# A planner's priorities replaced by searched offsets per kind of operation, in a kernel whose five engines follow one written-out plan

## The chip, the cores and the metric

One core of one Trainium2 chip. The metric is device time in microseconds (us) of one execution; the kernel before took 943.68 us as the median of three runs (940.2, 943.68, 949.0). Its profiled execution, from which all rows below come, is another one: 950.11 us, with a span of 948.3 us from the first to the last instruction.

## The reference

Two branches read the same 2048 tokens of 448 channels, float32, and are summed with the input:

```python
x = A_q
xn = _layernorm(x, axis=-1)
return x + _A_ref(xn, A_k, A_v, A_shift_k, A_ssm_k, A_ssm_D) + _B_ref(xn, B_w_q, B_k1, B_k2, B_u, B_v)
```

Branch A is `xn * y`, where `y` is a causal convolution over all 2048 steps, channel by channel (computed with Fourier transforms of length 4096), of the product of a 4-tap convolution of `k` and `v`. Branch B is a lookup among 4096 experts by 16 heads:

```python
s1 = einsum("nhd,ed->nhe", q1, k1); s2 = einsum("nhd,ed->nhe", q2, k2)   # 64 + 64 scores per head
# the best 2 + 2, then the best 2 of the 4 sums -> 2 experts per head, softmax g
act = _gelu(einsum("nd,nhkd->nhk", xf, u[top_e]))
out = einsum("nhk,nhk,nhkd->nd", g, act, v[top_e])
```

So each token reads 32 rows of `u` and 32 of `v`, 65,536 rows of 3,584 bytes in all when both are kept side by side.

## The kernel before

**Tiles and batches.** The tokens are 16 tiles of 128. Of each tile the 32 experts of a token are taken in 8 *batches*, 128 batches in all. A batch is four gathers (line 536, on GpSimd), each of 128 rows of 3,584 bytes, into one of 5 places of `ring`. Then VectorE multiplies the four with the normalized tokens, which TensorE has spread into `xs` (`prod`, line 569); ScalarE sums each of the four products over the channels (`sum`, four times line 575) and applies gelu (line 577); GpSimd makes the coefficients (`co` line 583, `coef` line 582; from batch 104 on VectorE does so, `LATE`); and TensorE adds the weighted rows to `pv` (`val`, line 588). A place of the ring is free for the gathers of batch b when `val` of batch b-5 has read it. After 8 batches `pv` and the tile's input, loaded into `fo`, are added (`res` line 605 and `fold`) and stored.

**Experts' choice.** At the start the query weights are folded with the keys, head by head (`weights`: load `wq`, `pw` line 365, `ws`, `pt`, `whi`, `wlo`). For each tile `turn` transposes the tokens, `score` makes the scores, 4 times 11 matmuls (lines 427 to 431), VectorE finds maxima and their places (`mx`, `mi`, lines 436 and 443) and `pick` makes the indices (`idx`) and gates (`gat`, both line 512) that the gathers need.

**Convolution.** Its 112 groups of 4 channels go in two parts, 28 groups (while the scores run) and 84 groups (after them). Each part has three stages: `in0` and `in1` (`conv_in`: load 4 groups, line 305; the taps, lines 638 to 644; transforms `ps1`, line 655), `sp0` and `sp1` (`spectrum`: `psf` line 699 or 703, `hh`, products `pr` line 720 and `y` lines 727 and 728; `inverse`: `psu` lines 746 to 749, `tw` lines 767 and 771) and `out0` and `out1` (`conv_out`: `psz` line 789, `zt`, `fin` line 796, `gate` and `gateG` lines 807 and 812). The gated result of tiles 0 to 13 is added to the stored rows by 14 accumulating transfers from GpSimd (`accum`, line 944); tiles 14 and 15 add it in `fo` (`add`, line 951).

**What sets the order.** Every step is recorded by `op(engine, duration, function, reads, writes, key)`. `Plan.solve` then lets time run with those durations: whenever an engine is free it takes, of the operations whose inputs are ready, the one with the smallest `key`. The start times that come out give one order for the whole program, and each engine executes its own part of it strictly in that order, waiting at an instruction until its inputs are there. The keys are due times: `tb(b)` for batch b, `due(T)` for the scores of tile T, `span(name, f)` for the fraction f of a stage of the convolution, each with a small constant. GpSimd's gathers and other operations alternate where both are ready. Three banks of PSUM are handed out in the planned order. A gather also waits for the matmul that the plan has ended by 0.5 us before it (`o.pace`).

The functions that the change touches:

Of the kernel before, what the change touches and what calls it, by code (L numbers as in the profile page):

```python
# [18 lines left out]
S, D, H, E = 2048, 448, 16, 64  # L19
# [62 lines left out]


class Op:
    __slots__ = ("eng", "dur", "fn", "deps", "users", "key", "acq", "rel", "nb", "start", "end", "name", "left", "avail", "pace", "last")


class Slot:
# [3 lines left out]
class Plan:  # L92
# [4 lines left out]

    def __init__(self):
        self.ops, self.writer, self.readers = [], {}, {}
        self.free = {}  # L100

    def pool(self, name, n):
# [2 lines left out]
    def op(self, eng, dur, fn, r=(), w=(), key=0.0, acq=None, rel=None, nb=0.0, name="", after=()):  # L105
        o = Op()
        o.eng, o.dur, o.fn, o.key, o.acq, o.rel, o.nb, o.name = eng, dur, fn, key, acq, rel, nb, name
        o.deps, o.users, o.start, o.pace, o.last = set(after), [], None, None, None
        for k in r:
            if k in self.writer:  # L110
                o.deps.add(self.writer[k])
            self.readers.setdefault(k, []).append(o)
        for k in w:
            if k in self.writer:
                o.deps.add(self.writer[k])
            o.deps.update(self.readers.get(k, ()))
# [117 lines left out]
def one_pass(ctx, tc, x, wq, kk, uv, kvh, cst1, cst2, fq, out, flag):  # L234
# [214 lines left out]
    def pick(T, b0, b1, key, two=1):  # L449
# [59 lines left out]
        def put(dst, k):  # L509
            o = bank[s.i][:, :8 * nj].rearrange("p (r k u j) -> p k u r j", r=4, k=2, u=two)[:, k]  # L510
            J = slice(0, NB) if two > 1 else slice(2 * b0, 2 * b1)
            nc.scalar.activation(dst[:, T % 8:T % 8 + two, :, J], o, AF.Copy)
        tiles = [(T + u) % 8 for u in range(two)]
        half = range(4) if two > 1 else range(b0, b1)
        op("ACT", 0.2 + 0.008 * n, lambda: put(idx, 0), r=["pl"], w=[("idx", t, i) for t in tiles for i in half], key=key, name="idx")
        op("ACT", 0.2 + 0.008 * n, lambda: put(gat, 1), r=["pl"], w=[("gat", t, i) for t in tiles for i in half], key=key, rel=("bank", s), name="gat")


    landed = []
# [40 lines left out]
    def batch(T, j):  # L560
        b = NB * T + j
        k = tb(b)
        U = ring[:, b % RING, :, :D]
        aw = sm[:, 4 * (b % 4):4 * (b % 4) + 4]
        ge = sm[:, 16 + 4 * (b % 4):20 + 4 * (b % 4)]
        co = sm[:, 32 + 4 * (b % 4):36 + 4 * (b % 4)]
        u = [("U", b % RING, r) for r in range(4)]
        m = 4
        op("DVE", dve(m * D), lambda: nc.vector.tensor_mul(U[:, :m, :], U[:, :m, :], xs[:, :m, :D]), r=["xs"], w=u[:m], key=k, name="prod")  # L569
        for r in range(m, 4):  # L570
            op("DVE", 0.78, lambda r=r: nc.vector.scalar_tensor_tensor(U[:, r, :], xs[:, r, :D], 1.0, U[:, r, :], op0=ALU.mult, op1=ALU.mult,
                                                                      accum_out=aw[:, r:r + 1]),
               r=["xs"], w=[u[r], ("aw", b % 4, r)], key=k, name="dot")
        for r in range(m):
            op("ACT", 0.575, lambda r=r: nc.scalar.activation(U[:, r, :], U[:, r, :], AF.Copy, accum_out=aw[:, r:r + 1]),  # L575
               w=[u[r], ("aw", b % 4, r)], key=k, name="sum")
        op("ACT", 0.2, lambda: nc.scalar.activation(ge, aw, AF.Gelu_apprx_tanh), r=[("aw", b % 4, r) for r in range(4)], w=[("ge", b % 4)], key=k, name="gelu")

        ve, en, d0, d1 = (nc.vector, "DVE", 0.17, 0.3) if b >= LATE else (nc.gpsimd, "POOL", 0.22, 0.41)

        def coef():
            last_val(ve.tensor_mul(cc[b % 3], co[:, :, None].broadcast_to([P, 4, 32]), rep[:, None, :].broadcast_to([P, 4, 32])).ins, b - 3)  # L582
        op(en, d0, lambda: ve.tensor_mul(co, ge, gat[:, T % 8, :, j]), r=[("ge", b % 4), ("gat", T % 8, j // 2)], w=[("co", b % 4)], key=k - 40.0, name="co")
        op(en, d1, coef, r=[("co", b % 4), "c1"], w=[("cc", b % 3)], key=k - 40.0, name="coef")

        def val():
            for r in range(4):
                v = nc.tensor.matmul(pv[32 * r:32 * r + 32, :D], cc[b % 3][:, r, :], ring[:, b % RING, r, D:],  # L588
                                     start=(j == 0), stop=(j == NB - 1), tile_position=(0, 32 * r)).ins
                tc.declare_no_dep(v, group=GROUP + "s", reason="the coefficients come from all four gathered slots")  # L590
                if r < 3:
                    tc.add_to_no_dep_group(GROUP, v)
            vins[b] = v.name
        op("PE", 1.0, val, r=[("cc", b % 3)] + ([("pv", j - 1)] if j else []), w=[("V", b % RING, r) for r in range(4)] + [("pv", j)] + (["pv"] if j == 0 else []), key=k, name="val")


    ob = [S1[:, 0:D], S1[:, D:2 * D]]

    def fold(T):
        k = tb(NB * T + NB) + 1.0  # L600
        o = fo[:, :]
        last = NB * T + NB - 1
        load(o, x[T], MB * D, ["fo"], k - 12.0, nb=k - 16.0, name="xr")
        if T < T_OUT0:
            op("PE", 0.85, lambda: nc.tensor.matmul(pv[:, :D], ident, o, start=False, stop=False), r=["fo", "c1", ("pv", 0)], w=[("pv", NB)], key=k - 2.0, name="res")
            op("ACT", act(D), lambda: last_val(nc.scalar.activation(o, pv[:, :D], AF.Copy).ins, last), r=[("pv", j) for j in range(NB + 1)], w=["fo", "pv"], key=k, name="fold")
        else:
            op("DVE", dve(D), lambda: last_val(nc.vector.tensor_add(o, o, pv[:, :D]).ins, last), r=[("pv", j) for j in range(NB)], w=["fo", "pv"], key=k, name="fold")
        return o, k
# [167 lines left out]
    def conv_out(p, c, n, tc0, gv, k):  # L777
# [24 lines left out]
        def fv():  # L802
# [1 line left out]
        xv = XA[:, :, ch].rearrange("p t (c k) -> p t c k", k=CH)  # L804
        reads = [("fin", hf) for hf in range(len(halves))]
        wk = [("x", t) for t in range(tc0)]
        op("DVE", dve(CH * n * tc0), lambda: nc.vector.tensor_mul(xv[:, :tc0], fv()[:, :tc0], xv[:, :tc0]), r=reads, w=wk, key=k,
           rel=None if tc0 < NT else ("bank", s), name="gate")
        if tc0 < NT:
            def gg():  # L810
                return gv[0]()[:, :, gv[1] + CH * c:gv[1] + CH * (c + n)].rearrange("p t (c k) -> p t c k", k=CH)
            op("DVE", dve(CH * n * (NT - tc0)), lambda: nc.vector.tensor_mul(gg(), fv()[:, tc0:], xv[:, tc0:]), r=reads + [("x", t) for t in range(tc0, NT)],
               w=[("G", p)], key=k, rel=("bank", s), name="gateG")


    norm(0, 1, 1.0)
# [26 lines left out]
            pick(T - 1, 0, 4, k + 8.0, 2)  # L843

    def conv_first(name, parts):
        tot, done = sum(PARTS[p][1] for p in parts), 0
        for p in parts:
            for c in range(0, PARTS[p][1], BC):
                conv_in(p, c, span(name, done / tot))
                done += BC  # L850

    def conv_mid(name, parts):
        for ka in range(17):
            qs = [ka, 32 - ka] if ka < 16 else [16]
# [168 lines left out]
```

## Time and profile before

| | us |
|---|---|
| median of three runs | 943.68 |
| profiled execution | 950.11 |
| its span | 948.3 |
| GpSimd busy | 606.9 |
| TensorE busy (matmuls) | 707.8 |
| VectorE busy | 679.5 |
| ScalarE busy | 542.9 |
| idle time of GpSimd ahead of gathers | 300.2 |

The page of the profile gives busy time for each engine (PE is TensorE, PEld its weight loads, DVE VectorE, ACT ScalarE, POOL GpSimd, SP the engine that issues the plain loads and stores). A table by windows gives the same for stretches of the span, with the granted share of TensorE's clock and the share of time in which the 16 DMA engines carried packets. The view of waits sums the idle time ahead of a group of instructions by what ended it. The timeline lists instructions with start and duration. "Line" is always a line of the kernel before; the change moves line 305 to 339, 536 to 570, 569 to 603, 588 to 622 and so on.

### The profile page before, as it was taken

The page shows a single profiled execution, that of the slowest core. Times are in us where ns is not written, and L with a number is a line of the kernel's source. Part 1 is how long each engine was busy: PE and PEld are TensorE (multiplying, and loading weights), DVE is VectorE, ACT ScalarE, POOL GpSimd, SP SyncE. Part 2 cuts the span into 40 slices and gives each one's busy share as a digit, 9 for nine tenths or more (in the row PEclk, how much of TensorE's full clock was granted, in tenths as well). Part 3 has the DMA queues.
Part 4 walks back from the last instruction along what each step waited for, and adds up shares of the span by engine and source line. Part 5 has one row for each costly group of instructions (what it writes and reads, how often), then busy time and mean ns, then how long its engine had stood idle before and what let it go on. Part 6 is the DMA issues. An engine that isn't in the chain of part 4 may idle for free.

```text
span 948.3 us, 13985 instructions
## 1 busy us (share of the span) xinstructions
PE 707.8 (75%) x4070; PEld 412.8 (44%) x4070; DVE 679.5 (72%) x1592; ACT 542.9 (57%) x1800; POOL 606.9 (64%) x754
## 2 busy tenths in 40 slices
PE   4777688677868898879888685666677988877671
PEld 2343455444535565546465453443333433344440
DVE  3479786788757887778777856777778999944451
ACT  2346275545554556656473475556577887855551
POOL 0036567688756765665657577787876776665564
PEclk9887779799878998889979778778789999987855
DMA  9998668788978887897779879999999899988898
GB/s 327 327 345 321 189 216 293 250 306 290 320 255 304 301 273 265 289 325 245 246 272 334 291 261 338 365 341 369 345 324 312 295 322 330 325 294 301 290 284 189
DMA packets 72214, 281.46 MB, mean 297 GB/s; under 512 B 10816, under 2 KB 35648, under 8 KB 72128
## 3 DMA queue, kind: packets, MB, share of 16 engines
q0 software_dynamic: 42976, 238.13, 73.5%
q1 hardware_dynamic: 29152, 42.35, 13.2%
q8 instruction: 34, 0.56, 0.2%
q14 instruction: 52, 0.43, 0.1%
HBM read 273.55 MB, written 6.88 MB: 296 GB/s over the span
## 4 chain that ended last, share of the span: by engine, by line
PE 29%; DVE 19%; issue 18%; POOL 12%; DMA 10%; ACT 7%; another core or an unknown queue 3%; SPq 0%; DVEq 0%; POOLq 0%; ACTq 0%
POOL ring L536 9%; DMA ring<-in_uv_dram,idx 8%; PE pv L588 5%; DVE SC L436 5%; DVE ring L569 5%; PE bank L655 4%; ACT ring L575 3%; PE bank L427 2%; PE bank L796 2%; DMA R<-in_wq_dram 2%; PE bank L428 2%; PE bank L429 2%; POOL cc L582 2%; DVE SC L443 2%
## 5 line engine op out<-in xcount | busy, mean ns | idle before, releaser
L536 POOL DMA_INDIRECT ring<-in_uv_dram,idx x512 | 506.9, 990 | 300.2 <-issue 95.4
L575 ACT ACTIVATE ring<-ring 128x448 f32<-128x448 f32 x512 | 288.5, 567 | 85.6 <-DVE ring L569 70.2
L569 DVE TENSOR_TENSOR ring<-ring,xs 128x1792 f32<-128x1792 f32 x128 | 257.4, 2016 | 95.6 <-DMA ring<-in_uv_dram,idx 81.5
L588 PE MATMUL pv<-ring,cc 128*32 128x448 f32 x1024 | 145.4, 650 | 69.8 <-POOL cc L582 34.4
L436 DVE MAX8 SC<-bank 128x8 f32<-128x64 f32 x512 | 118.5, 231 | 47.9 <-PE bank L431 21.7
L655 PE MATMUL bank<-c,S 128*64 128x132 f32 x896 | 77.5, 329 | 30.8 <-ACT ring L575 8.8
L427 PE MATMUL bank<-WR,xh 128*128 128x512 f32 x192 | 89.4, 466 | 10.9 <-DVE xl L416 4.9
L575 ACT ACTIVATION_READ_ACCUMULATOR ring<-ring 128x1 f32 x512 | 97.1, 190 | 0.0
L655 PEld LDWEIGHTS bank<-c,S 128*64 128x64 f32 x896 | 63.7, 165 | 65.3 <-ACT ring L575 24.4
L429 PE MATMUL bank<-WR,xl 128*128 128x512 f32 x192 | 82.7, 431 | 3.1 <-issue 2.5
L428 PE MATMUL bank<-WR,xh 128*128 128x512 f32 x192 | 82.8, 431 | 0.8 <-DVE WR L386 0.8
L588 PEld LDWEIGHTS pv<-ring,cc 128*32 128x32 f32 x1024 | 22.3, 116 | 122.6 <-POOL cc L582 46.0
L703 PE MATMUL bank<-x1b,S 128*128 128x336 f32 x132 | 51.6, 496 | 12.6 <-ACT x1b L767 5.0
L427 PEld LDWEIGHTS bank<-WR,xh 128*128 128x128 f32 x192 | 40.5, 211 | 42.0 <-issue 17.5
L659 ACT ACTIVATE x1b<-bank 128x264 f32<-128x264 f32 x84 | 30.8, 388 | 44.0 <-PE bank L655 32.5
L714 ACT ACTIVATE S<-bank 64x112 f32<-64x112 f32 x132 | 34.0, 257 | 37.1 <-PE bank L699 16.3
L443 DVE FIND_INDEX8 SC<-SC,bank 128x8 uint32<-128x256 f32 x128 | 52.7, 424 | 0.0
L720 DVE TENSOR_TENSOR S<-bank,S 128x224 f32<-128x224 f32 (+1 forms) x66 | 40.5, 618 | 13.8 <-issue 4.0
L582 POOL TENSOR_TENSOR cc<-sm,c 128x128 f32<-128x128 f32 x104 | 48.2, 463 | 3.3
L746 PE MATMUL bank<-S,c 128*128 128x112 f32 x264 | 42.0, 322 | 6.7 <-issue 2.7
L429 PEld LDWEIGHTS bank<-WR,xl 128*128 128x128 f32 x192 | 40.6, 211 | 14.3 <-issue 2.9
L365 PE MATMUL bank<-R 128*64 128x448 f32 x128 | 31.8, 631 | 19.7 <-DMA R<-in_wq_dram 15.6
(130 smaller groups left out, 1020.1 us busy)
## 6 DMA issues: line engine op xcount, KB each, us to landing
R<-in_wq_dram SPq DMA_DIRECT2D x16, 896.0 KB
S<-in_kvh_dram SPq DMA_DIRECT2D x28, 400.0 KB
ring<-in_uv_dram,idx POOLq DMA_INDIRECT x512
S<-in_fq_dram SPq DMA_DIRECT2D x66, 64.0 KB
fo<-in_x_dram SPq DMA_DIRECT2D x16, 224.0 KB
out_dram<-fo SPq DMA_DIRECT2D x16, 224.0 KB
out_dram<-XA POOLq DMA_DIRECT2D x14, 224.0 KB
XA<-in_x_dram SPq DMA_DIRECT2D x2, 1344.0 KB
```

The source lines that it names most:

```text
L427: nc.tensor.matmul(o, xh[:, c, :], wh[:, c, ns], start=(c == 0), stop=False)
L428: nc.tensor.matmul(o, xh[:, c, :], wl[:, c, ns], start=False, stop=False)
L429: nc.tensor.matmul(o, xl[:, c, :], wh[:, c, ns], start=False, stop=False)
L436: nc.vector.max(mx[:, 8 * n + j, :] if safe else m2[:, m, 2 * j:2 * j + 8], bank[s.i][:, 64 * j:64 * j + 64])
L443: nc.vector.max_index(m4i[:, 2 * m + g, :], m2[:, m, 8 * g:8 * g + 8], bank[s.i][:, 256 * g:256 * g + 256])
L536: g = nc.gpsimd.indirect_dma_start(dst, None, uv, bass.IndirectOffsetOnAxis(ap=idx[:, T % 8, r, j:j + 1], axis=0)).ins
L569: op("DVE", dve(m * D), lambda: nc.vector.tensor_mul(U[:, :m, :], U[:, :m, :], xs[:, :m, :D]), r=["xs"], w=u[:m], key=k, name="prod")
L575: op("ACT", 0.575, lambda r=r: nc.scalar.activation(U[:, r, :], U[:, r, :], AF.Copy, accum_out=aw[:, r:r + 1]), w=[u[r], ("aw", b % 4, r)] ...
L582: last_val(ve.tensor_mul(cc[b % 3], co[:, :, None].broadcast_to([P, 4, 32]), rep[:, None, :].broadcast_to([P, 4, 32])).ins, b - 3)
L588: v = nc.tensor.matmul(pv[32 * r:32 * r + 32, :D], cc[b % 3][:, r, :], ring[:, b % RING, r, D:], start=(j == 0), stop=(j == NB - 1), tile_ ...
L655: nc.tensor.matmul(o[64 * i:64 * i + 64, w * j:w * j + w], src, f1[:, i, :], start=True, stop=True, tile_position=(0, 64 * i))
L703: op("PE", 0.95 * n / 448 + 0.05, lambda t=t, sl=sl: nc.tensor.matmul(bank[sl.i][:, :n], fmb[u], x1[p][:, :, q, t, :], start=True, stop=True),
```

## The change: four offsets for each kind of operation

Each operation gets a group, its name and, in the convolution, its stage (`psf@sp1`). For 94 groups a table `RANK` holds four numbers. Over the keys that the group has in the kernel, from its smallest to its largest, the four numbers are interpolated linearly and added to the key. Durations, `solve`, tiling, buffers and every instruction stay. Three dependencies are added that follow the written order wherever keys could now turn it round: `gat` after `idx`, `gateG` after `gate`, and the last `val` of a tile after `res`. Loading `fo` and `res` move out of `fold` into `residual`, which is recorded after the tile's first batch.

```diff
+RANK = {
+    "DMAc1": (-94.0, -79.0, 73.0, 37.0), "DMAc2": (-7.0, 6.5, 6.5, 7.5), ...
+    "DMAkk": (-103.0, -41.0, -70.5, -15.5), "DMAkvh@in0": (-81.5, -81.5, -84.5, -13.0), ...
+    "gather": (1331.0, 1476.0, 2096.5, 2406.5), "gelu": (-52.5, -91.0, -73.5, -120.5), ...
...
+}
@@ pick
-        op("ACT", 0.2 + 0.008 * n, lambda: put(idx, 0), ...)
-        op("ACT", 0.2 + 0.008 * n, lambda: put(gat, 1), ...)
+        ahead = op("ACT", 0.2 + 0.008 * n, lambda: put(idx, 0), ...)
+        op("ACT", 0.2 + 0.008 * n, lambda: put(gat, 1), ..., after=(ahead,), name="gat")
@@ batch
-        op("PE", 1.0, val, r=[("cc", b % 3)] + ([("pv", j - 1)] if j else []), ...)
+        op("PE", 1.0, val, r=[("cc", b % 3)] + ([("pv", j - 1)] if j else []) + ([("pv", NB)] if j == NB - 1 and T < T_OUT0 else []), ...)
@@ experts
             batch(T, j)
+            if j == 0:
+                residual(T)
@@ one_pass, before the plan is solved
+    for o in pl.ops:
+        if o.group in RANK:
+            (a, b), v = ends[o.group], RANK[o.group]
+            w = (o.key - a) / (b - a) * (len(v) - 1) if b > a else 0.0
+            i = min(len(v) - 2, int(w))
+            o.key = o.key + (v[i] * (1 - (w - i)) + v[i + 1] * (w - i))
```

Every engine's order changes, mostly over short distances. Three places follow at which the prediction looks.

The first is the start of SP's queue, which issues the loads: `c` are constants, `XA` tokens (128x448 is one tile), `kk` the keys, `wq` the query weights of a head. Before:

```order
L305 DMA c_67<-in_cst_dram 128x269
L305 DMA XA<-in_x_dram 128x448
L305 DMA R_92<-in_kk_dram 128x256
L305 DMA R_92<-in_wq_dram 128x4x448 x4
L305 DMA XA<-in_x_dram 128x448
L305 DMA XA<-in_x_dram 128x2x448
L305 DMA XA<-in_x_dram 128x6x448 x2
L305 DMA R_92<-in_wq_dram 128x4x448 x8
```

and with the change:

```order
L339 DMA XA<-in_x_dram 128x448 x2
L339 DMA c_67<-in_cst_dram 128x269
L339 DMA XA<-in_x_dram 128x2x448
L339 DMA R_92<-in_wq_dram 128x4x448 x4
L339 DMA R_92<-in_kk_dram 128x256
L339 DMA XA<-in_x_dram 128x6x448 x2
L339 DMA R_92<-in_wq_dram 128x4x448 x6
```

Three tiles of tokens moved ahead of the weights, and the keys behind the first four heads.

The second is VectorE where the second part of the convolution goes from `in1` to `sp1`. Before, from the product of batch 88 (`ring<-ring,xs`) on; 128x1024 to 128x4x64 are the taps of four groups, 128x448 is the `fold` of a tile, and 128x672 with two of 64x336 the products of a spectrum:

```order
L569 TENSOR_TENSOR ring<-ring,xs 128x4x448
L638 TENSOR_TENSOR S_72<-S_72 128x1024
L639 TENSOR_TENSOR S_72<-S_72 128x4
L642 TENSOR_TENSOR S_72<-S_72 128x4x128
L643 TENSOR_TENSOR S_72<-S_72 128x4x64
L644 TENSOR_TENSOR S_72<-S_72 128x4x64
L608 TENSOR_TENSOR fo<-fo,pv 128x448
L569 TENSOR_TENSOR ring<-ring,xs 128x4x448 x2
L720 TENSOR_TENSOR S_72<-bank_84,S_72 128x672
L727 TENSOR_TENSOR Y<-S_72 64x336
L728 TENSOR_TENSOR Y<-S_72 64x336
```

With the change, from the product of batch 86 on:

```order
L603 TENSOR_TENSOR ring<-ring,xs 128x4x448
L677 TENSOR_TENSOR S_72<-S_72 128x1024
L678 TENSOR_TENSOR S_72<-S_72 128x4
L681 TENSOR_TENSOR S_72<-S_72 128x4x128
L682 TENSOR_TENSOR S_72<-S_72 128x4x64
L683 TENSOR_TENSOR S_72<-S_72 128x4x64
L603 TENSOR_TENSOR ring<-ring,xs 128x4x448 x2
L759 TENSOR_TENSOR S_72<-bank_84,S_72 128x672
L766 TENSOR_TENSOR Y<-S_72 64x336
L767 TENSOR_TENSOR Y<-S_72 64x336
L647 TENSOR_TENSOR fo<-fo,pv 128x448
```

The last taps moved from batch 88 to batch 86, and the first spectrum from behind batch 90 to behind batch 88.

The third is the end of GpSimd's queue, gathers and accumulating transfers (`out_dram<-XA`). Before:

```order
L582 TENSOR_TENSOR cc_75<-sm,c_67 128x128
L536 DMA ring<-in_uv_dram,idx 128x896 x83
L944 DMA out_dram<-XA 128x448
L536 DMA ring<-in_uv_dram,idx 128x896
L944 DMA out_dram<-XA 128x448
L536 DMA ring<-in_uv_dram,idx 128x896
L944 DMA out_dram<-XA 128x448
L536 DMA ring<-in_uv_dram,idx 128x896
L944 DMA out_dram<-XA 128x448 x11
```

and with the change:

```order
L570 DMA ring<-in_uv_dram,idx 128x896
L616 TENSOR_TENSOR cc_75<-sm,c_67 128x128
L570 DMA ring<-in_uv_dram,idx 128x896 x87
L991 DMA out_dram<-XA 128x448 x14
```

The last three gathers moved ahead of the first accumulating transfer.

More of the change, by code (lines that the diff above doesn't have):

```diff
@@ L84 @@
 class Op:
-    __slots__ = ("eng", "dur", "fn", "deps", "users", "key", "acq", "rel", "nb", "start", "end", "name", "left", "avail", "pace", "last")
+    __slots__ = ("eng", "dur", "fn", "deps", "users", "key", "acq", "rel", "nb", "start", "end", "name", "left", "avail", "pace", "last", "group")
 class Slot:
@@ L99, in __init__ @@
         self.ops, self.writer, self.readers = [], {}, {}
+        self.stage = ""
         self.free = {}
@@ L108, in op @@
         o.deps, o.users, o.start, o.pace, o.last = set(after), [], None, None, None
+        o.group = name + self.stage
         for k in r:
@@ L216 @@
 LEAD = 0.5
+RANK = {
+    "DMAc1": (-94.0, -79.0, 73.0, 37.0), "DMAc2": (-7.0, 6.5, 6.5, 7.5), "DMAfm@sp0": (30.0, 7.0, -47.0, -79.5), "DMAfm@sp1": (73.5, 60.5, 36.0, 65.5),
+    "DMAkk": (-103.0, -41.0, -70.5, -15.5), "DMAkvh@in0": (-81.5, -81.5, -84.5, -13.0), "DMAkvh@in1": (-191.5, -155.5, -149.0, -60.0),
+    "DMAwq": (-349.0, -13.0, -74.5, -56.0), "DMAx": (-60.0, -81.0, -76.5, -62.0), "DMAxr": (-53.0, -70.5, -83.0, -83.0),
+    "E": (42.0, -43.5, -42.5, -60.0), "SPc1": (-21.5, -0.5, -69.5, 79.5), "SPc2": (11.0, -5.0, 25.0, -46.0), "SPfm@sp0": (-65.0, -64.0, 57.0, -59.5),
+    "SPfm@sp1": (10.0, 10.0, 10.0, 10.0), "SPkk": (34.0, -18.5, -60.0, -42.5), "SPkvh@in0": (-3.5, -22.5, 12.5, 12.5),
+    "SPkvh@in1": (-2.5, 13.0, 28.0, 46.5), "SPwq": (12.0, -0.5, 0.0, 5.5), "SPx": (-101.0, -66.0, -1.0, 130.5),
+    "SPxr": (-145.5, -112.0, -137.0, -134.0), "accum": (-82.0, -105.5, -82.0, -92.0), "accumD": (23.5, 8.0, -32.0, 8.0),
+    "add": (-135.0, -70.5, -116.0, -106.0), "bad": (-32.5, -27.0, -36.0, 6.5), "co": (-0.5, -164.5, -973.5, -827.5),
+    "coef": (60.5, 162.5, -318.0, -288.5), "es": (37.0, 13.0, 31.0, 21.0), "fin@out0": (-10.5, -10.5, -10.5, -10.5),
+    "fin@out1": (-20.5, 44.0, 31.0, -1.5), "flag": (-91.5, -120.0, -136.5, -221.0), "fold": (59.0, 10.0, 142.5, 122.5),
+    "gat": (-8.0, -41.5, -41.5, 1.0), "gate@out0": (-55.5, -102.5, -55.5, 26.0), "gate@out1": (-37.5, -27.0, -27.5, 11.0),
+    "gateG@out0": (-148.0, -206.0, -16.0, -29.5), "gateG@out1": (29.0, 93.5, 26.0, 63.5), "gated": (-57.5, -43.0, -164.5, -244.0),
+    "gather": (1331.0, 1476.0, 2096.5, 2406.5), "gelu": (-52.5, -91.0, -73.5, -120.5), "hh@sp0": (-133.5, -173.5, -144.5, -233.5),
+    "hh@sp1": (-72.0, -91.5, -56.0, -48.0), "idx": (-183.0, -101.0, -44.5, -92.5), "join": (-131.5, -45.0, -25.5, -24.5),
[7 rows of a table added]
+    "sc": (1.0, 1.0, -0.0, 6.5), "spread": (-3.0, -43.5, -104.5, 12.0), "stats": (138.0, 123.5, 136.5, 91.0), "store": (117.5, 205.5, 234.5, 276.0),
+    "storeD": (35.5, 39.0, -18.0, -91.5), "sum": (-13.5, -3.5, -14.0, -3.5), "tap1@in0": (7.0, -69.0, -47.0, -47.0),
+    "tap1@in1": (0.0, -11.0, 0.0, 0.0), "tap2@in0": (-99.5, -114.5, -86.0, -78.5), "tap2@in1": (-99.0, -62.5, -76.5, -36.5),
+    "taps@in0": (-16.0, -3.0, 22.0, -1.5), "taps@in1": (163.0, 251.0, 69.0, 52.5), "th": (1.0, -3.0, -40.5, -40.5), "tw@sp0": (26.0, 11.0, 43.0, 3.0),
+    "tw@sp1": (-17.0, 56.5, 50.5, -145.5), "val": (30.0, 0.5, 3.5, 48.5), "whi": (-362.0, -283.5, -250.0, -143.0),
[4 rows of a table added]
+}
@@ L514, in pick @@
         half = range(4) if two > 1 else range(b0, b1)
-        op("ACT", 0.2 + 0.008 * n, lambda: put(idx, 0), r=["pl"], w=[("idx", t, i) for t in tiles for i in half], key=key, name="idx")
-        op("ACT", 0.2 + 0.008 * n, lambda: put(gat, 1), r=["pl"], w=[("gat", t, i) for t in tiles for i in half], key=key, rel=("bank", s), name="gat")
+        ahead = op("ACT", 0.2 + 0.008 * n, lambda: put(idx, 0), r=["pl"], w=[("idx", t, i) for t in tiles for i in half], key=key, name="idx")
+        op("ACT", 0.2 + 0.008 * n, lambda: put(gat, 1), r=["pl"], w=[("gat", t, i) for t in tiles for i in half], key=key, rel=("bank", s), after=(ahead,), name="gat")
     landed = []
@@ L593, in val, with residual @@
             vins[b] = v.name
-        op("PE", 1.0, val, r=[("cc", b % 3)] + ([("pv", j - 1)] if j else []), w=[("V", b % RING, r) for r in range(4)] + [("pv", j)] + (["pv"] if j == 0 else []), key=k, name="val")
+        op("PE", 1.0, val, r=[("cc", b % 3)] + ([("pv", j - 1)] if j else []) + ([("pv", NB)] if j == NB - 1 and T < T_OUT0 else []), w=[("V", b % RING, r) for r in range(4)] + [("pv", j)] + (["pv"] if j == 0 else []), key=k, name="val")
     ob = [S1[:, 0:D], S1[:, D:2 * D]]
+    def residual(T):
+        k = tb(NB * T + NB) + 1.0
+        o = fo[:, :]
+        load(o, x[T], MB * D, ["fo"], k - 12.0, nb=k - 16.0, name="xr")
+        if T < T_OUT0:
+            op("PE", 0.85, lambda: nc.tensor.matmul(pv[:, :D], ident, o, start=False, stop=False), r=["fo", "c1", ("pv", 0)], w=[("pv", NB)], key=k - 2.0, name="res")
     def fold(T):
@@ L602, in fold @@
         last = NB * T + NB - 1
-        load(o, x[T], MB * D, ["fo"], k - 12.0, nb=k - 16.0, name="xr")
         if T < T_OUT0:
-            op("PE", 0.85, lambda: nc.tensor.matmul(pv[:, :D], ident, o, start=False, stop=False), r=["fo", "c1", ("pv", 0)], w=[("pv", NB)], key=k - 2.0, name="res")
             op("ACT", act(D), lambda: last_val(nc.scalar.activation(o, pv[:, :D], AF.Copy).ins, last), r=[("pv", j) for j in range(NB + 1)], w=["fo", "pv"], key=k, name="fold")
@@ L806, in conv_out @@
         wk = [("x", t) for t in range(tc0)]
-        op("DVE", dve(CH * n * tc0), lambda: nc.vector.tensor_mul(xv[:, :tc0], fv()[:, :tc0], xv[:, :tc0]), r=reads, w=wk, key=k,
+        ahead = op("DVE", dve(CH * n * tc0), lambda: nc.vector.tensor_mul(xv[:, :tc0], fv()[:, :tc0], xv[:, :tc0]), r=reads, w=wk, key=k,
            rel=None if tc0 < NT else ("bank", s), name="gate")
@@ L812, in conv_out @@
             op("DVE", dve(CH * n * (NT - tc0)), lambda: nc.vector.tensor_mul(gg(), fv()[:, tc0:], xv[:, tc0:]), r=reads + [("x", t) for t in range(tc0, NT)],
-               w=[("G", p)], key=k, rel=("bank", s), name="gateG")
+               w=[("G", p)], key=k, rel=("bank", s), after=(ahead,), name="gateG")
     norm(0, 1, 1.0)
@@ L845, in conv_first @@
     def conv_first(name, parts):
+        pl.stage = "@" + name
         tot, done = sum(PARTS[p][1] for p in parts), 0
@@ L850, in conv_first @@
                 done += BC
+        pl.stage = ""
     def conv_mid(name, parts):
+        pl.stage = "@" + name
         for ka in range(17):
@@ L859, in conv_mid @@
                 inverse(p, ka, ys, k + 3.0)
+        pl.stage = ""
     def conv_last(name, parts, tc0, gv):
+        pl.stage = "@" + name
         tot, done = sum(PARTS[p][1] for p in parts), 0
@@ L868, in conv_last @@
                 done += n
+        pl.stage = ""
     def join(keys, new, fn=None):
@@ L952, in one_pass @@
         store(T, o, k + 1.0, ["fo"])
+    ends = {}
+    for o in pl.ops:
+        a, b = ends.get(o.group, (o.key, o.key))
+        ends[o.group] = min(a, o.key), max(b, o.key)
+    for o in pl.ops:
+        if o.group in RANK:
[3 more added lines that the diff above has]
+            o.key = o.key + (v[i] * (1 - (w - i)) + v[i + 1] * (w - i))
     order = pl.solve()
```

11 rows, old and new, of the table RANK are left out of this document.

## The prediction, made before the changed kernel ran

> **What bounds the kernel now.** First the page, for the whole span.
>
> ```profile
> span 948.3 us, 13985 instructions
> PE 707.8 (75%) x4070; PEld 412.8 (44%) x4070; DVE 679.5 (72%) x1592; ACT 542.9 (57%) x1800; POOL 606.9 (64%) x754
> DMA packets 72214, 281.46 MB, mean 297 GB/s; under 512 B 10816, under 2 KB 35648, under 8 KB 72128
> ```
>
> No engine is full. The median run (943.68 us) is 0.7% below the profiled execution (950.11 us, span 948.3); I work out a difference against the span and take it from the median. The next view gives busy time by windows. I put the borders where the product of every eighth batch starts, so that a window holds one tile's 8 batches; I call them blocks 0 (58.8:131.5) to 15 and the end.
>
> ```profile
> 0.00:58.80 58.80, 39.80 (x196) 17.83 (x196) 28.78 (x120) 20.01 (x54) 8.45 (x14) 0.91 0.96 341
> ...
> 248.80:308.10 59.30, 43.56 (x229) 26.92 (x225) 41.20 (x121) 32.43 (x119) 37.93 (x49) 0.84 0.85 288
> 308.10:362.50 54.40, 47.11 (x246) 30.24 (x247) 44.28 (x134) 30.82 (x112) 36.07 (x49) 0.88 0.86 290
> ...
> 630.40:683.00 52.60, 33.04 (x314) 19.56 (x312) 39.44 (x49) 30.79 (x103) 42.59 (x49) 0.76 0.98 358
> 683.00:737.80 54.80, 42.40 (x210) 21.60 (x211) 43.18 (x53) 41.36 (x124) 39.20 (x51) 0.89 0.93 320
> 737.80:784.10 46.30, 41.53 (x169) 17.15 (x168) 44.33 (x57) 39.73 (x117) 34.25 (x44) 1.00 0.91 309
> ```
>
> After the window's length come PE, PEld, DVE, ACT and POOL busy, granted clock, DMA share, GB/s. Four stages have four limits. Up to 58.8 us the loads fill the DMA engines (0.96). Blocks 1 to 7 (131.5 to 532.3) have none: in 248.8:308.1 PE is busy 43.6 of 59.3 us, the DMA share is 0.85, and the rest is engines waiting for each other. Block 10 (630.4:683.0) is DMA: 0.98 at 358 GB/s. Block 12 is VectorE: 44.33 of 46.3. Who waits for whom in the stage without a limit:
>
> ```profile
> DVE ring L569 <- DMA ring<-in_uv_dram,idx: 81.5, 38, 6.2
> POOL ring L536 <- ACT gat L512: 70.7, 5, 43.9
> ACT ring L575 <- DVE ring L569: 70.2, 36, 8.8
> POOL ring L536 <- PE pv L588: 33.3, 24, 5.0
> ```
>
> (us, times, longest). The cycle is that of the ring: gathers wait 33.3 us for `val` to free a place, products wait 81.5 us for gathered rows.
>
> **The change, part by part.** It adds and removes no work, so each term is work moved from a place where it sets the pace to one where it doesn't, or back.
>
> *The head.* The page's engines start with the loads:
>
> ```profile
> 1.67 0.42 SPq L305 DMA_DIRECT2D R<-in_kk_dram  x1
> 2.13 2.30 SPq L305 DMA_DIRECT2D R<-in_wq_dram  x4
> 4.48 8.16 SPq L305 DMA_DIRECT2D XA<-in_x_dram  x4
> ...
> 8.43 5.09 PE L365 MATMUL bank<-R 128*64 128x448 f32 x16 [8.43 <-DMA R<-in_wq_dram]
> ...
> 26.96 3.26 PE L365 MATMUL bank<-R 128*64 128x448 f32 x8 [7.17 <-DMA R<-in_wq_dram]
> ```
>
> The first fold of the weights needs `wq` of one head and `kk`. It started at 8.43; the order now puts three tiles (0.69 MB) and three more heads (2.75 MB) ahead of `kk`. 3.44 MB at the 341 GB/s of the window are 10.1 us: it starts at about 18.5. But PE stood still for 7.17 us before the fifth head, whose bytes ahead are the same 8.5 MB as before, so it had 8.43 + 7.17 = 15.6 us of idle time and now has 18.5: **+2.9 us**. Bounds: 0, if the four heads' work then fits in before the fifth lands, and +10.1, if nothing of the old idle time is used.
>
> *Blocks 0 to 7.* For both orders I counted each engine's operations per block and multiplied by durations of the trace: a score is 11 matmuls,
>
> ```profile
> 33.99 0.47 PE L427 MATMUL bank<-WR,xh 128*128 128x512 f32 x1
> ...
> 36.37 0.40 PE L431 MATMUL bank<-WR,xl 128*128 128x512 f32 x1
> ...
> 744.92 0.83 PE L703 MATMUL bank<-x1b,S 128*128 128x336 f32 x2
> ...
> L536 POOL DMA_INDIRECT ring<-in_uv_dram,idx x512 | 506.9, 990 | 300.2 <-issue 95.4 <-ACT gat L512 70.7 <-PE pv L588 33.3
> ```
>
> 2.78 us from 33.99 to 36.77; a gather is 0.99 and 0.3 of issue (`issue` ends most gaps); and so on. The largest sum of a block is its bound:
>
> | block | 1 | 2 | 3 | 4 | 5 | 6 | 7 | sum |
> |---|---|---|---|---|---|---|---|---|
> | before | 53.1 | 51.3 | 52.7 | 51.6 | 44.9 | 53.8 | 53.1 | 360.5 |
> | change | 50.4 | 51.7 | 48.2 | 46.1 | 47.5 | 54.5 | 54.7 | 353.1 |
>
> Blocks 3 and 4 lose most: of their scores, 8 and 7 (PE places ahead of `val`), 7 and 6 are left, with two spectra and three inverse steps fewer; block 5, which had PE and VectorE idle, takes them. **-7.4 us**. Block 0 takes in a 12th score and its transposes, 2.78 + 0.75: **+3.5**. Bounds for the two: the blocks lasted 400.8 us over a bound of 360.5, so if the waits alone set the pace it is 0; if the surplus shrinks in proportion, -8.2.
>
> *Blocks 8 to 10* stay: 32 gathers (14.7 MB), 8 loads of convolution inputs (3.3) and the tile's own load and store (0.46) are 18.4 MB, at 358 GB/s 51.5 us of the 52.6. **0**, whatever the order; the cover is DMA, and without it POOL's 44.9 us would be next.
>
> *Blocks 11 to 13.* Two sets of taps and one spectrum's product now come before batch 88. Their rows:
>
> ```profile
> L720 DVE TENSOR_TENSOR S<-bank,S 128x672 f32<-128x672 f32 x33 | 28.2, 853 | 4.5 <-ACT S L718 1.6 <-PE bank L703 0.9 <-ACT ring L575 0.7
> L638 DVE TENSOR_TENSOR S<-S 128x1024 f32<-128x1024 f32 x28 | 34.5, 1232 | 9.6 <-PE bank L655 5.7 <-remote 3.4 <-issue 0.4
> L642 DVE TENSOR_TENSOR S<-S 128x512 f32<-128x512 f32 x21 | 14.5, 690 | 0.0
> L644 DVE TENSOR_TENSOR S<-S 128x256 f32<-128x256 f32 x28 | 11.9, 425 | 2.8 <-POOL S L643 2.0
> ```
>
> Taps are 1.23 + 0.69 + two of 0.43 + a small one of 0.21 = 3.0 us, twice 6.0, with 0.85 is 6.8 us off VectorE where it is the bound. On PE, blocks 11 and 12 lose 10 spectrum matmuls of 0.83 and block 13 gains 7, still under VectorE. Block 13 then has PE 1.4 us above its old bound: **-5.4**; bounds 0 (block 11, 54.8 long at 43.18 busy, is not wholly VectorE's) and -12 (were PE the bound).
>
> *The end.* Last gathers, accumulating transfers and products:
>
> ```profile
> 917.84 1.03 POOL L944 DMA_DIRECT2D out_dram<-XA  x1
> 920.21 1.06 POOL L536 DMA_INDIRECT ring<-in_uv_dram,idx  x1 [1.34 <-ACT sm L577]
> ...
> 925.52 1.08 POOL L536 DMA_INDIRECT ring<-in_uv_dram,idx  x1 [0.90 <-ACT sm L577]
> 926.52 10.01 POOL L944 DMA_DIRECT2D out_dram<-XA  x11
> ...
> 931.85 2.02 DVE L569 TENSOR_TENSOR ring<-ring,xs 128x1792 f32<-128x1792 f32 x1 [6.18 <-DMA ring<-in_uv_dram,idx]
> ```
>
> Three gathers stood among 14 accumulating transfers, and the last product waited 6.18 us. The transfers began at 917.84 and the span ended at 948.3, 30.5 us later. In the new order all gathers are ahead: 14 transfers of 0.91 are 12.7, and from the last issue (936.53) to the end were 11.8, together 24.5, so -6. Against it the last 8 batches now hold three more half chunks of the convolution's output, about 1 us each on PE: **-3**. Bounds -6 and 0.
>
> *Waits inside the blocks.* For each wait I counted the work that the order places on the waiting engine between the step waited for and the waiting step. Where that cover is shorter than the step takes, the difference is a stall. For gathers behind `val` (1.8 us) the shortage falls from 41.4 us in 31 batches to 18.3 in 17. For products behind gathers (5.15 us, between the 5.0 of the chain's row below and the 6.3 from 925.52 to 931.85) it falls from 106.6 to 83.4, of which 15 in blocks 8 to 10, where DMA gives nothing back; 8.1 are left.
>
> ```profile
> 915.38 5.00 DMA ring<-in_uv_dram,idx
> ```
>
> Against the measured waits: 33.3 x 23.1/41.4 = 18.6 and 81.5 x 8.1/106.6 = 6.2, in all 24.8. But sums behind products on ScalarE lose cover, their shortage rises from 99 to 122 us. So from -24.8 to +23. ScalarE is idle for 405 us and can wait; GpSimd's waits hold the transfers. I take half of the gain, **-12.4**, since a wait removed is often followed by the next.
>
> The added dependencies cost nothing, since `idx`, `gate` and `res` stood ahead in both orders. `fo` is loaded behind the store of the tile before it, as it was.
>
> Sum: +2.9 - 7.4 + 3.5 + 0 - 5.4 - 3 - 12.4 = -21.8 us, and 943.68 - 21.8 = 921.9, rounded **922 us** (928 for an execution like the profiled one).
>
> **The rivals.** *DMA takes it back: no change.* 281.46 MB at 358 GB/s are 786 us; batches that come faster raise the share elsewhere to block 10's and the transfers stretch. For it: shares of 0.91 to 0.98 in the windows shown from 630 us on. Against it: 0.85 in blocks 3 and 4, where I count most. Only what is not hidden by transfers is left, +6.4 of head and block 0, -5.4 of blocks 11 to 13 and -3 at the end: 942 us.
>
> *ScalarE hands the stall on: slower.* In batches 0 to 63 the sums' shortage rises from 35.9 to 64.4 us, 28.5. Behind a waiting sum stand the evictions of scores and spectra, which hold one of three banks, and PE waits for a bank. If all of it reaches PE, the other terms (-9.4) leave +19.1: 963 us. It decides against the change from 19 us on, that is if more than two thirds arrive. For it: ScalarE already waits 70.2 us for products. Against it: ScalarE is the least busy engine.
>
> *Transfers have room: faster still.* Then the 15 us of blocks 8 to 10 come too, down to POOL's 44.9 us per block: 907 us. Against it: a share of 0.98. The Trainium skill's page "DMA: Bandwidth & Descriptors" (Anatomy of one DMA — SWDGE (gpsimd) path) fits a transfer as 2.0 us and its bytes at 436e3 per us; by that rate, as an estimate, the 18.4 MB would be 42 us. No run here shows more than the 369 GB/s of the page's best slice.
>
> *It reorders nothing that matters.* Five of the seven bounds of the table differ by under 3 us. Against it: the three places shown in the change. I count this with no change.
>
> **How the numbers follow.** My forecast (905 to 934) has 0.47, transfers with room 0.10, so faster by over 1% has 0.57; DMA takes it back 0.24; ScalarE 0.19. One per cent, 9.4 us, is about what runs between 940.2 and 949.0 can tell from no change. The range is 896 to 957: below, the forecast with all 24.8 us of waits (-12.4 more) and transfers with room; above, two thirds of the way into the slower case. That leaves out about 2 in 10.
>
> **What would show it.** TensorE's first matmul near 18.5 us, and the first gather, which waited 43.9, up to 5 us later. Waits of gathers for `val` near 15 us, of products near 75. Blocks 3 and 4 together under 106 us (113.7 before), blocks 11 and 12 under 96 (101.1), 8 to 10 within 3 us. From the first accumulating transfer to the end about 25 us. The prediction is wrong if blocks 1 to 7 last 400 us or more, or if waits of ScalarE for products rise by over 20 us and PE's idle time with them.

## The result, and the profile after

| | before | change | |
|---|---|---|---|
| median, us | 942.61 (4 runs) | 917.07 (4 runs, 910.15 to 919.07) | ratio 0.971, 95% interval 0.963 to 0.978 |
| profiled span | 948.3 | 917.3 | -31.0 |

The change makes the kernel 2.9% faster; 922 was forecast and 917 measured. Where the time went is another matter: the parts differ from the forecast by more than their sum does. The page after, span and busy time:

```profile
span 917.3 us, 13979 instructions
PE 680.2 (74%) x4070; PEld 398.4 (43%) x4070; DVE 682.0 (74%) x1592; ACT 545.8 (60%) x1800; POOL 605.2 (66%) x754
```

Busy time of VectorE, ScalarE and GpSimd stands still, as no work was added or removed; TensorE's is lower by 28 us at a higher granted clock (0.885 against 0.839). The table by windows of the change, with borders where the product of every eighth batch starts as in the prediction (window and length, then PE, PEld, DVE, ACT, POOL busy, granted clock, DMA share, GB/s):

```profile
0.00:59.20 59.20, 37.16 (x191) 16.44 (x191) 37.40 (x151) 22.02 (x55) 8.41 (x14) 1.00 0.96 337
...
231.80:279.70 47.90, 40.45 (x219) 25.95 (x217) 40.19 (x117) 30.14 (x108) 34.72 (x46) 0.93 0.92 319
279.70:337.90 58.20, 46.11 (x245) 28.98 (x246) 42.10 (x122) 32.66 (x117) 39.33 (x55) 0.88 0.86 293
...
597.50:650.00 52.50, 31.25 (x346) 20.48 (x344) 38.65 (x51) 31.67 (x109) 40.50 (x49) 0.90 0.97 352
650.00:701.30 51.30, 41.69 (x170) 18.79 (x171) 43.12 (x53) 40.22 (x118) 38.80 (x50) 0.93 0.94 334
701.30:747.20 45.90, 37.18 (x152) 16.43 (x152) 39.84 (x49) 39.76 (x120) 35.28 (x46) 0.93 0.94 324
747.20:799.30 52.10, 40.93 (x161) 18.46 (x162) 45.68 (x69) 37.90 (x111) 34.47 (x37) 0.97 0.92 325
```

Blocks 1 to 7, block 8 and the last stage in one row each, first before, then after:

```profile
131.50:532.30 400.80, 322.55 (x1808) 207.79 (x1807) 307.85 (x908) 220.45 (x792) 274.87 (x360) 0.89 0.83 282
532.30:578.50 46.20, 33.36 (x247) 20.30 (x248) 27.18 (x33) 28.59 (x99) 30.60 (x40) 0.71 0.84 288
882.70:948.30 65.60, 32.60 (x173) 18.11 (x173) 25.14 (x38) 25.79 (x85) 37.01 (x40) 0.60 0.90 252
```

```profile
132.20:492.70 360.50, 293.45 (x1690) 187.24 (x1689) 291.89 (x838) 214.42 (x763) 261.90 (x344) 0.92 0.89 305
492.70:543.40 50.70, 35.83 (x276) 21.91 (x277) 34.82 (x63) 30.64 (x104) 35.16 (x46) 0.76 0.86 291
846.10:917.30 71.20, 37.79 (x204) 22.93 (x204) 26.72 (x44) 27.67 (x88) 37.10 (x40) 0.62 0.85 234
```

Blocks 1 to 7 gained 40.3 us, more than the whole. The rest lost 9.3: 4.5 in block 8, 5.6 in the last stage. Blocks 11 to 13, where 5.4 were forecast, went from 149.1 to 149.3.

What the engines no longer wait for, in the view of waits. Before (scores for maxima, gelu for `co`, the convolution's matmuls for their evictions):

```profile
POOL sm L583 <- ACT sm L577: 22.3, 14, 5.7
DVE SC L436 <- PE bank L431: 21.7, 11, 5.6
ACT S L714 <- PE bank L699: 16.3, 6, 8.6
ACT R L767 <- PE bank L746: 10.5, 2, 9.4
```

and after, with the two cycles of the ring that the prediction counted:

```profile
ACT ring L609 <- DVE ring L603: 56.0, 34, 4.1
DVE ring L603 <- DMA ring<-in_uv_dram,idx: 51.6, 29, 4.2
POOL ring L570 <- PE pv L622: 16.1, 18, 2.3
ACT S L753 <- PE bank L738: 12.9, 10, 3.1
DVE SC L470 <- PE bank L465: 4.6, 5, 2.1
ACT R L806 <- PE bank L785: 3.5, 3, 2.4
POOL sm L617 <- ACT sm L611: 1.9, 2, 1.1
```

Of the waits that the prediction counted, that of gathers for `val` came out as forecast, 16.1 us (33.3 before, about 15 forecast). Products wait 51.6 us for gathered rows (81.5 before, near 75 forecast), and ScalarE's wait for products, where a rise was counted, fell from 70.2 to 56.0. Waits that it did not count fell as well: `co` for gelu by 20.4, maxima for scores by 17.1, and the two rows of evictions by 10.4. No engine waits longer at one place after the head than the last addition for its input, 12.3 us, shown further down. The longest single waits fell too, from 5.0 to 2.3 us for the gathers and from 8.6 to 3.1 for the evictions.

### The profile page after: what moved, and what is told of

Same layout as the page of the kernel before. It is cut to its first block, busy times and chain, and to the rows that moved or that the text cites. A ratio compares the mean times of both kernels' runs of the same rounds, so it can differ in the third digit from the quotient of the medians.

```text
span 917.3 us, 13979 instructions
## 1 busy us (share of the span) xinstructions
PE 680.2 (74%) x4070; PEld 398.4 (43%) x4070; DVE 682.0 (74%) x1592; ACT 545.8 (60%) x1800; POOL 605.2 (66%) x754
## 4 chain that ended last, share of the span: by engine, by line
PE 39%; DVE 16%; issue 16%; DMA 10%; POOL 10%; ACT 6%; another core or an unknown queue 1%; SPq 1%; DVEq 0%; POOLq 0%; ACTq 0%
POOL ring L570 8%; PE pv L622 8%; DVE ring L603 5%; DMA ring<-in_uv_dram,idx 4%; PE bank L694 4%; ACT ring L609 3%; PE bank L461 3%; DVE SC L470 3%; PE bank L742 3%; PE bank L462 3%; PE bank L463 3%; PE bank L785 2%; PE bank L835 2%; DMA fo<-in_x_dram 2%; PE xs L591 2%
## 5 line engine op out<-in xcount | busy, mean ns | idle before, releaser
L603 DVE TENSOR_TENSOR ring<-ring,xs 128x1792 f32<-128x1792 f32 x128 | 257.4, 2015 | 66.0 <-DMA ring<-in_uv_dram,idx 51.6
L622 PE MATMUL pv<-ring,cc 128*32 128x448 f32 x1024 | 141.6, 632 | 64.8 <-POOL cc L616 28.5
L694 PE MATMUL bank<-c,S 128*64 128x132 f32 x896 | 74.9, 318 | 32.7 <-ACT R L698 6.9
L461 PE MATMUL bank<-WR,xh 128*128 128x512 f32 x192 | 86.2, 449 | 15.6 <-DVE SC L470 4.9
L694 PEld LDWEIGHTS bank<-c,S 128*64 128x64 f32 x896 | 60.3, 158 | 66.2 <-ACT ring L609 22.3
L462 PE MATMUL bank<-WR,xh 128*128 128x512 f32 x192 | 78.9, 411 | 0.5 <-DVE WR L420 0.5
L463 PE MATMUL bank<-WR,xl 128*128 128x512 f32 x192 | 78.6, 409 | 0.0
L461 PEld LDWEIGHTS bank<-WR,xh 128*128 128x128 f32 x192 | 38.3, 200 | 43.9 <-issue 9.6
L677 DVE TENSOR_TENSOR S<-S 128x1024 f32<-128x1024 f32 x28 | 34.6, 1235 | 22.6 <-DMA S<-in_kvh_dram 10.6
L835 PE MATMUL bank<-c,S 128*128 128x64 f32 x168 | 33.5, 359 | 21.8 <-ACT S L830 18.3
L616 POOL TENSOR_TENSOR cc<-sm,c 128x128 f32<-128x128 f32 x104 | 45.4, 438 | 2.8
```

The lines of the kernel that those rows point to most:

```text
L461: nc.tensor.matmul(o, xh[:, c, :], wh[:, c, ns], start=(c == 0), stop=False)
L462: nc.tensor.matmul(o, xh[:, c, :], wl[:, c, ns], start=False, stop=False)
L463: nc.tensor.matmul(o, xl[:, c, :], wh[:, c, ns], start=False, stop=False)
L694: nc.tensor.matmul(o[64 * i:64 * i + 64, w * j:w * j + w], src, f1[:, i, :], start=True, stop=True, tile_position=(0, 64 * i))
L835: nc.tensor.matmul(bank[s.i][:, 64 * j:64 * j + 64], z[:, P * (j - a):P * (j - a) + P], f3, start=True, stop=True)
```

## The experiments

The theory after this was A: the order within blocks 1 to 7 makes the whole gain. Against it stood a loan that later stages pay back (B), a higher clock (C) and balance in later stages (D). Each profile is one execution, and a stretch of it has no interval. Kernels on one chip share their runs of the kernel before; that took 910.7 us on the chip of the first four, 945.4 on that of the next and 940.5 on that of the last, so only ratios are compared across them.

**Without the table.** `RANK = {}`; the dependencies and the loading of `fo` stay changed.

> The change without its table: only the three added dependencies and the loads and additions of the tiles' inputs recorded after the first batch. Theory A (the offsets make the gain, in blocks 1 to 7): 943, within 5 us of before. Rival R (the earlier recording of the inputs makes a good part of it, since TensorE waited for them 10 us): 932 or less.

911.1 against 910.7 us, ratio 0.999 (0.995 to 1.003). R falls; the table makes the gain.

**Offsets for half of the program.**

```diff
-        if o.group in RANK:
+        if o.group in RANK and o.key < SC_END:      # early; late has >=
```

> The offsets only for operations whose own due time lies before 383.1, the end of the scores, which is about blocks 0 to 7. Theory A (the whole gain is made by the order inside blocks 1 to 7): batch 64 starts near 493 us instead of 532, the rest takes the 416 us that it took before, so the profiled span is near 909 and the median near 907, somewhat better than the whole change at 917. Rival B (the gain in blocks 1 to 7 is a loan that later stages with the old order pay back): 930 or more. Rival C (a higher granted clock made it, 0.885 against 0.839, and not the order): the span follows the clock, near 945 at 0.84.

> The offsets only for operations due at or after 383.1. Theory A: no gain, 943 to 952, since the later stages of the change took 425 us against 416. Rival D (balance in blocks 11 to 13 and all gathers ahead of the accumulating transfers, as the prediction had it, -8.4 us): near 934.

Early: 0.968 (0.959 to 0.977), the whole gain. Late: 0.993 (0.989 to 0.996). That is a small gain where A had none, and the interval just takes in D's 0.990, so A's "no gain" is missed and D isn't excluded. The absolute times expected don't apply on this faster chip. In the late profile the two terms of D come near their forecast sizes, 5.4 and 3 us. Blocks 11 to 13 lasted 140.4 us, against 145.8 without the table:

```profile
651.00:796.80 145.80, 122.35 (x539) 55.50 (x535) 131.23 (x177) 120.95 (x357) 107.97 (x131) 0.96 0.93 329
```

```profile
644.30:784.70 140.40, 116.16 (x482) 51.42 (x475) 128.41 (x172) 117.17 (x345) 110.83 (x134) 0.98 0.97 351
```

The last two stages took 112.9 us (784.7 to 897.6) against 115.1 (796.8 to 911.9). In the whole change neither is there. On this chip, the kernel without the table and the one with early offsets, batches 8 to 64 and 64 to the end:

```profile
129.30:505.40 376.10, 311.53 (x1809) 201.28 (x1807) 306.39 (x908) 220.29 (x794) 273.25 (x361) 0.91 0.87 300
505.40:911.90 406.50, 287.13 (x1819) 154.29 (x1819) 286.12 (x385) 265.16 (x834) 288.13 (x335) 0.82 0.92 318
```

```profile
125.10:473.00 347.90, 293.66 (x1716) 190.49 (x1717) 294.50 (x855) 216.10 (x767) 265.09 (x348) 0.93 0.91 322
473.00:875.60 402.60, 284.04 (x1826) 151.78 (x1825) 288.29 (x398) 266.97 (x840) 289.68 (x338) 0.83 0.93 322
```

28.2 us come from batches 8 to 64, 4.2 from before and 3.9 from after. Batches 64 to the end, in nearly the old order, keep the gain: B falls for these. A smaller loan is paid inside the first stretch: the product of batch 56 starts 43.2 us earlier than without the table (408.7 against 451.9), that of batch 64 only 32.4. The likely reason is that the batches had run ahead of the convolution's first part and the scores, which have to be finished there: TensorE is busy for 53.3 us in that block, against 45.4 without the table.

**The keys first, by leaving six groups out of the table.** `SPkk`, `SPc1`, `SPx` and their `DMA` groups keep their old keys.

> The change, with the loads of constants, tokens and keys at the start in the old places (the keys ahead of the weights). The prediction's term for the head: first matmul near 8.4 instead of 18.1 us, 914 against 917. Rival E (the idle time before the fifth head comes back in its place and the later gathers hide the rest): 917, no difference.

929.3 us, ratio 1.024 (1.015 to 1.033): slower than before. The first matmul came at 15.8 us, not near 8.4: the keys stood ahead again, and it waited for the weights. The first gather came at 44.4, earlier than the change's 47.3, and the first product at 59.7 instead of 59.2. The kernel lost later, in batches 40 to 48 for one, which took 60.7 us (46.4 in the change's profile). Neither expectation speaks of that. Six groups of loads had other keys, the plan was solved again, and every engine's order came out otherwise. This is no test of the head; the next experiment of it moves one entry of a finished order.

**The change again, and three families.** Early offsets for the scores and the choice alone, for the batches (gather to store) alone, and for the rest (convolution, weights, loads) alone:

```diff
-        if o.group in RANK:
+        if o.group in SCORE and o.key < SC_END:     # BATCH; neither of both
```

> The change itself once more, to stand on the same chip as the next three. Its ratio to before was 0.971. If the offsets for blocks 0 to 7 alone (0.968) are all of it, this is again 0.966 to 0.976.

> Offsets in blocks 0 to 7 only for the operations of the scores and the choice of experts. Theory A1 (the gain is that scores stand up to two ahead and no longer pile up in blocks 3 and 4): two thirds or more of the 0.968 of all early offsets, that is 0.978 or less. Theory A2 (it is the cycle of the ring: gathers, products, sums, coefficients, val): 0.99 to 1.00. Rival A3 (only all families together fit): 0.99 to 1.01.

> Offsets in blocks 0 to 7 only for the operations of the batches, from gather to val, fold and store. A1: 0.99 to 1.00. A2: 0.978 or less, with the gathers' wait for val about half of before. A3: 0.99 to 1.01, or slower.

> Offsets in blocks 0 to 7 only for the convolution's first part, the folding of the weights and the loads. A1 and A2: 0.99 to 1.01. A3: the same, or slower. If neither A1 nor A2 nor A3: 0.98 or less here, which would mean that the convolution's work between scores and batches sets the pace.

| early offsets for | ratio (interval) | first product | batches 0 to 64 | 64 to the end |
|---|---|---|---|---|
| none (before, as shown above) | 1 | 58.8 | 473.5 | 416.0 |
| whole change | 0.973 (0.966 to 0.980) | 58.4 | 427.9 | 425.9 |
| scores | 0.996 (0.992 to 0.999) | 71.0 | 440.4 | 424.8 |
| batches | 1.019 (1.012 to 1.026) | 63.1 | 467.1 | 426.5 |
| convolution, weights, loads | 0.982 (0.975 to 0.988) | 58.4 | 453.3 | 413.9 |

The change repeats its ratio. By ratios A1 and A2 fall, and A3 doesn't fit the convolution's 0.982, which is close to the 0.98 set for "none of the three". The stretches tell more: between batches 0 and 64 the scores' offsets gain 33 us, the convolution's 20, the batches' 6, together 59 where the whole change gains 46. A2, the ring's own cycle on which my term of waits rested, is the smallest. These aren't net gains: from batch 64 on the scores' kernel takes 9 us more than before, the batches' 11 and the whole change 10, so part of what they gain is probably work left for later. The scores lose 12 us ahead of the first product: their first gather waited 60.3 us for its indices (46.2 with the change).

```profile
POOL ring L570 <- ACT gat L546: 63.1, 3, 60.3
```

**Scores with the weights and loads of the head.** Is that loss due to scores overtaking the weights?

> Offsets due before 383.1 for the scores and choice of experts, and for the folding of the weights and the loads of the head; none for batches and convolution. The scores alone had lost 12 us before the first product and gained 33 us between batches 0 and 64. Theory A1' (that loss is the weights, which the earlier scores overtake, and the gain is the scores'): first product near 59 us, batch 64 near 500 or earlier, ratio to before 0.972 to 0.980. Rival A3' (the families fit only together): first product near 59, but batch 64 at 512 or later, 0.985 or more.

0.979 (0.975 to 0.983), first product at 57.6, batch 64 at 493.1: A1'. Batches 0 to 64 in one row:

```profile
57.60:493.10 435.50, 350.91 (x2007) 222.28 (x2009) 346.72 (x994) 254.03 (x903) 305.66 (x397) 0.91 0.87 296
```

435.5 us, 38 less than before, without any offset on a batch or the convolution; 9 of them come back after batch 64 (424.6 against 416.0).

Which wait this removes isn't settled by the families. With the scores' offsets alone, maxima wait 7.8 us for scores between batches 0 and 64 (20.7 before), but with the batches' alone, which gain 6 us there, only 6.4. And with the convolution's alone, which gain 20, the evictions wait longer for their matmuls than in the kernel before (16.3 and 10.5 in the rows above), not less:

```profile
ACT R L806 <- PE bank L785: 21.9, 6, 8.7
ACT S L753 <- PE bank L738: 20.6, 8, 4.8
```

**C, the clock.** The early offsets came with a higher granted clock, too, so their time alone doesn't decide. Single runs at the same clock show how much is left without it, roughly. The scores with the head took 923.4 us at 0.857, the kernel before on that chip 939.2 at 0.857: 16 of the 20 us are left. The early offsets took 887.1 us at 0.880, the kernel without the table, as slow as before, 903.7 at 0.881: 17 of 32. Nor does TensorE's busy time set the span: in the profiles of the keys moved and of the buffer of its own, below, it is 689.6 and 679.4 us, in spans of 904.0 and 904.9. C is not the main cause, but it isn't nothing either. A straight line through the 13 runs of the kernel before on the second chip, at 0.835 to 0.866, falls by about 3 us for 0.01 of clock. By that, as an estimate, the step from 0.839 to 0.885 goes with some 14 of the 31 us. Whether the clock shortens the run or fewer stalls raise the clock stays open.

**The keys moved in the finished order.**

```diff
     order = pl.solve()
+    keys = next(o for o in order if o.name == "SPkk")
+    order.remove(keys)
+    order.insert(next(i for i, o in enumerate(order) if o.name == "SPwq"), keys)
```

> The change with one entry of the finished order moved: the keys are loaded before the first query weights. No other instruction moves on its engine. The prediction's term for the head (+2.9): first matmul near 10.5 instead of 18.1 us, first gather near 44.5 instead of 47.3, 2 to 3 us faster than the change, 0.970 where it has 0.973. Rival E: the first matmuls start earlier and wait for the fifth head instead; first gather at 47 and no difference.

0.968 (0.964 to 0.972), not to be told from the change's 0.973 (0.966 to 0.980). The first matmul hardly moved:

```profile
17.27 6.24 PE L399 MATMUL bank<-R 128*64 128x448 f32 x16 [17.27 <-DMA R<-in_wq_dram]
```

It now waits for the weights, not the keys, and the first gather came at 47.1, as in rival E. The built order has the first four heads' loads as 3, 2, 1, 0, where they read 0, 1, 2, 3 before: head 0, which is folded first, lands last. The rows of the order that I had read print all four as one.

**A buffer of its own for the last tile.** The change's last addition waits for its input, which waits for the store of tile 14. Accumulating transfers, that store (895.98), the load and the last additions:

```profile
890.53 12.59 POOL L991 DMA_DIRECT2D out_dram<-XA  x14 [0.74 <-DVE G L851]
...
895.98 0.34 SPq L651 DMA_DIRECT2D out_dram<-fo  x1
...
902.19 0.33 SPq L339 DMA_DIRECT2D fo<-in_x_dram  x1
910.50 0.62 DVE L647 TENSOR_TENSOR fo<-fo,pv 128x448 f32<-128x448 f32 x1 [12.34 <-DMA fo<-in_x_dram]
```

```diff
+    def fo_of(T):
+        return (S1[:, 2048:2048 + D], "fo2") if T == NT - 1 else (fo[:, :], "fo")
```

> The change with the input of the last tile loaded into a buffer of its own, so that it need not wait for the store of tile 14. The 12.3 us in which the last addition waited for that load go. Theory T (the accumulating transfers, landing until 912.5 of 917.3, are right behind as the end): 2 us faster than the change. Rival U (the load is the end): 9 to 10 us faster, as the last addition would start near 900 instead of 910.5.

0.966 (0.963 to 0.969). The wait is gone, and the span ends at 904.9:

```profile
879.48 12.56 POOL L994 DMA_DIRECT2D out_dram<-XA  x14
...
891.03 0.62 DVE L650 TENSOR_TENSOR S<-S,pv 128x448 f32<-128x448 f32 x1 [1.84 <-PE pv L622]
```

The last addition starts 11.6 us after the first accumulating transfer instead of 20.0, and the end comes 25.4 us after it instead of 26.8: 1.4 us. The same kernel without this buffer but with the keys moved, on the same chip, ended at 904.0, 26.8 us after its first transfer. T holds by these stretches; a gain in the whole time is not shown.

**Early offsets, keys moved.**

> The offsets for blocks 0 to 7 alone (0.968 on another chip) with the keys loaded before the first weights, as the likely best version. Theory A: 0.963 to 0.970, and from batch 64 to the end the 406 to 416 us of the old order. Rival B' (the later offsets are worth something of their own, 0.993 alone): no better than the whole change, 0.973.

0.966 (0.962 to 0.970), inside A's range, with 409.7 us from batch 64 on. The best ratios, 0.966 to 0.968, belong to the early offsets with and without the keys moved, to the change with the keys moved and to the buffer of its own. All lie within the interval of the change, so none is shown to beat it, and B' isn't excluded.

## Why the prediction was right, and where it wasn't

That the sum came out right is in part luck. In the two profiles the terms, forecast and measured, are: head and block 0 +6.4 and +0.7; blocks 1 to 7 with the waits -19.8 and -40.3; blocks 8 to 10 0 and +6.6; blocks 11 to 13 -5.4 and +0.2; the last two stages -3 and +1.8. The place of the gain and its sign were right, its size there was half of the true one, and three terms behind it that failed took part of the error back. Three of the signs that the prediction set were missed besides: blocks 3 and 4 took 106.1 us (under 106 was set), blocks 11 and 12 97.2 (under 96), and blocks 8 to 10 moved by 6.6 (within 3).

**The head, +2.9.** The first matmul came at 18.09 where 18.5 was forecast, and the first gather at 47.3 instead of 45.0. It cost 0.4 us at the first product. The reason given, the keys, was not enough: head 0's own weights stood as far back, which moving the keys alone showed.

**Block 0, +3.5.** 73.0 against 72.7 us: the work moved in found idle time, at a granted clock of 0.98 instead of 0.74.

**Blocks 1 to 7, -7.4 and most of -12.4.** This is the term that was mis-sized: -40.3 measured, -46 in a second execution. The bound by the busiest engine fell from 360.5 to 353.1 as counted, and what the blocks lasted beyond it from 40.3 to 7.4. So what I had as waits was worth 33 us and not 12. The bound is counted in durations of the kernel before, at its clock, so shorter matmuls are part of the 33: the one of a score at line 429 took 431 ns on average before and 409 after. Two parts failed. I counted three kinds of wait, all in the ring's cycle, and that family's offsets alone gain 6 us; those of the scores and of the convolution gain 33 and 20. Which of their waits these gains come from stays open. And I halved what I had counted, expecting another wait behind each, where the products' wait alone fell by 29.9 us over the span, for which 6.2 were set.

**Blocks 8 to 10, 0.** Blocks 9 and 10 lasted 106.6 us (104.5 before), block 10 at 0.97 of DMA and 52.5 us. Block 8 lost 4.5 at the turn between the convolution's parts, which I had as DMA's and which isn't.

**Blocks 11 to 13, -5.4.** Nothing. VectorE's busy time in them fell by 2.5 us (131.2 to 128.6), not 6.8, and block 11's 3.5 us came back in block 13 as 4.1. With the late offsets alone the term was there (140.4 against 145.8), so the reasoning isn't refuted, but the plan of the whole change doesn't show it.

**The end, -3.** From the first accumulating transfer to the end 26.8 us, 25 forecast, 30.5 before. But the last two stages together lost 1.8: from the start of block 14 to the first transfer it took 91.2 us instead of 85.7. The longer list of convolution outputs there, for which 3 us were set, is the likely reason; no run isolates it.

**The rivals.** DMA did not take the gain back; its share in block 3 rose from 0.85 to 0.92. ScalarE's wait for products fell from 70.2 to 56.0 us (36.2 and 37.2 in blocks 1 to 7), so the slower case did not begin. That transfers have more room was not seen in blocks 8 to 10: block 10 stayed at 352 GB/s. The Trainium skill's page "DMA: Bandwidth & Descriptors" (Anatomy of one DMA — SWDGE (gpsimd) path) fits a transfer as 2.0 us and its bytes at 436e3 per us. No run here shows that rate; the highest of the 40 slices of any page is 396 GB/s, in two of the experiments. The 369 GB/s which the prediction gave as the most in any slice were exceeded, though, by 391 in one slice of the page after. The lower end of the range, 896, is 894.5 by the sum given for it.

## What to carry to other kernels

When in-order engines share a plan, count the cover of every kind of wait in the stage that has no limit of its own, in the side work too: here blocks 1 to 7 came within 7.4 us of the bound counted for the busiest engine, where half of the counted waits had been expected to come back. Add up the forecast term by term against the profile, as a right sum can hide wrong terms. Compare runs at the same granted clock before a gain is put down to the order. Compare single parts of a searched order by moving entries of the finished order; taking some of its priorities away solves another plan, here one 2.4% slower than the start. And read which buffer a row moves, not only how many rows there are.

## What was not expected of the hardware

The same kernel took 910.7 us as the median on one chip and 940.5 to 945.4 on two others. The ratios of the early offsets on the first (0.968) and of the same with the keys moved on another (0.966) agree all the same, within their intervals.
